# Decode block with attention and MLP: implied semaphore waits left out, a finer last piece of the second MLP matrix, one store from ACT

## The chip, the cores and the metric

The kernel runs on one core of a Trainium2 chip. The metric is the device time in microseconds of one execution; of several runs the median is given, with the lowest and the highest. Beside these runs one execution is profiled; its trace gives the rows shown below.

## What is computed

Eight tokens (B = 8, one position each, D = 576) go through an attention block and an MLP, and a gate mixes the two:

```
g = sigmoid((x * gate_w).sum(-1))
q = x @ wq                                  # 32 heads of 128, 16 heads of K and V
p = softmax(q . k / sqrt(128))              # over the last 2048 of 8192 cached positions
a = (p . v) @ wo                            # wo: 4096 x 576
b = gelu(layernorm(x) @ w1 + b1) @ w2 + b2  # w1: 576 x 4608, w2: 4608 x 576
out = g * a + (1 - g) * b
```

All inputs are bfloat16. The cached keys and values that are read (2 x 64 MiB) are most of what is moved; the four weight matrices make up most of the rest.

## The kernel before

**The planner.** The kernel is written as a list of operations (`_Op`), each with an engine, a function that issues it, the operations that it depends on (`deps`), operations that it must only be issued after (`after`), and a guessed cost. `_Plan.schedule()` (line 62) plays the list through with these costs, takes at each step the operation that can start first, and so fixes the order of each engine: ACT, POOL, DVE, PE, and SP, which issues almost all transfers. It also gives each operation a planned start and end (`t0`, `t1`). Then each operation that another one depends on gets a number on its engine's semaphore (`milestone`, lines 129 to 139); a transfer counts 16 on a semaphore of its own.

**The waits.** `emit` (line 141) walks one engine's order. For each dependency it issues a `wait_ge` (line 153), unless this engine has already waited for the same semaphore at that value or a higher one (`known`). It doesn't see that a wait for one operation may already say that another is done: because the other stands earlier on the same engine, or because the one waited for has itself waited for the other. An operation with several dependencies on one engine, in rising order, so gets a wait for each of them.

**The stream.** Transfers run through nine slots of 2 MB in SBUF. A K unit (line 635, 32 of them) is four batches of one KV head: one transfer, two transposes on DVE (line 653), score matmuls (line 667) into four PSUM banks. Four K units make a group; `softmax` (line 595) then takes the maxima over the row (598), brings three quarters of the partitions to the first (601), takes maxima of these (602, 603, 604), writes the scaled negative to four places (607), and runs four exponentials on ACT (612) and four transposes on DVE (617); the sums go through 620 to 623 and 629. A V unit (line 679, 32) is one transfer, 16 matmuls (690), an evacuation by ACT (696), eight small matmuls that gather the result (701), and after every second unit another ACT evacuation (711) and a product on POOL (719). After eight V units `wo_chunk` (722) brings in a quarter of `wo`, arranges rows by matmul (734), evacuates them by ACT (738) and adds 16 matmuls of the projection.

The stream's order is five K units, then K and V in turn with the `wo` quarters in between; when the K units are used up, V units 27 to 31, the last quarter of `wo`, the bias (line 746) and the second MLP matrix `w2` in four blocks (`m2_chunk`, line 754). A block has 9 weight rows for each partition and takes 18 matmuls. The first three blocks come by one transfer each; the last comes in pieces of 4, 3 and 2 rows, each with its own semaphore. Projection, bias and `w2` all add into one PSUM bank through `AccGroup` (line 543, matmuls at line 552): each weight row is a pair of matmuls of 288 columns, the left half of the output to partitions 0 to 7 and the right half to partitions 32 to 39.

**The end.** When all groups have added up, DVE copies the left half (line 779) and ACT the right half (780) to `out_sb`, at partitions 0 and 32, and each half is stored by a transfer of its own, from SP and from ACT (782). SP waits for both (`final_wait`, 783).

Each engine has one queue in order. A wait blocks what stands behind it on its engine.

Of the kernel before, what the change touches and what calls it, by code (L numbers as in the profile page):

```python
# [6 lines left out]
BF = mybir.dt.bfloat16  # L7
# [5 lines left out]
ENGS = ("sp", "act", "pool", "dve", "pe")  # L13
# [25 lines left out]
class _Plan:  # L39
# [10 lines left out]
    def add(self, eng, fn, deps=(), name=None, cost=0.1, after=(), prio=0):  # L50
        op = _Op(eng, fn, deps, name, cost, after=after, prio=prio)
        op.idx = len(self.all)
        self.all.append(op)
        return op

    def dma(self, eng, fn, semkey, nbytes, deps=(), name=None, after=(), prio=0):
        op = _Op(eng, fn, deps, name, self.DMA_ISSUE, after=after, is_dma=True, dma_sem=semkey, nbytes=nbytes, prio=prio)
        op.idx = len(self.all)
        self.all.append(op)
        return op  # L60

    def schedule(self):
        n = len(self.all)
        done = [False] * n
        eng_free = {e: 0.0 for e in ENGS}
        dma_free = 0.0
        remaining = set(range(n))
        npred = [0] * n
        succ = [[] for _ in range(n)]
        for op in self.all:  # L70
            preds = set(d.idx for d in op.deps) | set(d.idx for d in op.after)
            npred[op.idx] = len(preds)
            for p in preds:
                succ[p].append(op.idx)
        ready = [i for i in range(n) if npred[i] == 0]
        count = 0
        while ready:
            best = None
            best_key = None
            for i in ready:  # L80
                op = self.all[i]
                r = 0.0
                for d in op.deps:
                    r = max(r, d.t1 + self.SEM_LAT)
                for d in op.after:
                    r = max(r, d.t0)
                est = max(eng_free[op.eng], r)
                key = (est - 0.2 * op.prio, -op.prio, i)
                if best_key is None or key < best_key:
                    best_key = key  # L90
                    best = i
            op = self.all[best]
            ready.remove(best)
            est = max([eng_free[op.eng]] + [d.t1 + self.SEM_LAT for d in op.deps] + [d.t0 for d in op.after])
            op.t0 = est
            if op.is_dma:
                eng_free[op.eng] = est + op.cost
                if op.nbytes < 65536:
                    op.t1 = est + 0.4 + self.DMA_LAT
                else:  # L100
                    start = max(est + 0.4, dma_free)
                    dma_free = start + op.nbytes / self.DMA_BW
                    op.t1 = dma_free + self.DMA_LAT
            else:
                op.t1 = est + op.cost
                eng_free[op.eng] = op.t1
            op.pos = len(self.order[op.eng])
            self.order[op.eng].append(op)
            done[best] = True
            count += 1  # L110
            for s_ in succ[best]:
                npred[s_] -= 1
                if npred[s_] == 0:
                    ready.append(s_)
        assert count == n, "dependency cycle in plan"
        self.makespan = max(op.t1 for op in self.all)
        prev = None
        for op in self.order["pool"]:
            narrow = op.name.startswith("qr")
            if prev is not None and narrow != prev.name.startswith("qr"):  # L120
                op.deps.append(prev)
            prev = op
        cnts = {}
        for e in ENGS:
            for op in self.order[e]:
                if op.is_dma:
                    cnts[op.dma_sem] = cnts.get(op.dma_sem, 0) + 1
                    op.dma_val = 16 * cnts[op.dma_sem]
        needed = set()
        for op in self.all:  # L130
            for d in op.deps:
                if not d.is_dma:
                    needed.add(d.idx)
        for e in ENGS:
            c = 0
            for op in self.order[e]:
                if op.idx in needed:
                    c += 1
                    op.milestone = c
# [32 lines left out]
def build_kernel(nc, A_x, A_k_cache, A_v_cache, A_wq, A_wo, B_x, B_w1, B_b1, B_w2, B_b2, gate_w, out):  # L172
    B, Sq, D = A_x.shape
# [12 lines left out]
    FC, FJ = 4, 9  # L186
# [6 lines left out]
    JN = D // NJ  # L193
    BIG = 1.0e9
    x2 = A_x.rearrange("b s d -> (b s) d")
    out2 = out.rearrange("b s d -> (b s) d")

    with ExitStack() as es:
# [5 lines left out]
        def req(name, nelem, dt, align=64):  # L204
            sz = 2 if dt == BF else 4
            o = aoff[0] + ARENA_BASE
            o = (o + align - 1) // align * align - ARENA_BASE
            R[name] = (o, nelem, dt)
            aoff[0] = o + nelem * sz
# [35 lines left out]
        req("oX", 2 * WO_CH * WO_CH * 8, BF)  # L245
        req("oP", 2 * WO_CH * 8, BF)
        req("o32", 2 * 16, F32)
        req("out_sb", JN, BF)
        req("PT", 2 * 2048, BF)
        req("P", 2048, BF)  # L250
        req("osb", 2 * 512, F32)
# [24 lines left out]
        def view(name, parts=128):  # L276
            o, n, dt = R[name]
            a = arena[0:parts, o // 2: o // 2 + (n * (2 if dt == BF else 4)) // 2]
            if dt == F32:
                a = a.bitcast(F32)  # L280
            return a
# [31 lines left out]
        out_sb = view("out_sb")  # L313
# [10 lines left out]
        def slot(s):  # L324
            return RAW[:, s * SE:(s + 1) * SE]
# [11 lines left out]
        ps = es.enter_context(nc.psum_tensor("ps", [128, 8, 512], F32))  # L337
# [5 lines left out]
        BK_ACC = 7  # L343
# [6 lines left out]
        add, dma = P.add, P.dma  # L350
# [43 lines left out]
        for s in range(2):  # L394
            o_xz.append(add("dve", (lambda s=s: lambda e: e.tensor_copy(xz[:, s, :].rearrange("p (k z) -> p k z", z=2)[:, :, s], x_sb[:, 512:576]))(),  # L395
                            deps=dx + [o_xz0], name="xz%d" % s, cost=0.12))
# [12 lines left out]
        for s in range(2):  # L409
            o_yz.append(add("dve", (lambda s=s: lambda e: e.tensor_copy(yz[:, s, :].rearrange("p (k z) -> p k z", z=2)[:, :, s], y_bf[:, 512:576]))(),  # L410
                            deps=[o_y, o_yz0], name="yz%d" % s, cost=0.12))
# [30 lines left out]
        def b1ev_fn(e):  # L442
# [5 lines left out]
                   deps=[o_dga, o_dgb, o_onesf], name="g_pe", cost=0.4, after=[o_yTp])  # L448
# [7 lines left out]
        for q in range(4):  # L456
            o_i32.append(add("dve", (lambda q=q: lambda e: e.tensor_copy(i32[32 * q:32 * q + 32, :], ident[32 * q:32 * q + 32, 32 * q:32 * q + 32]))(),
                             deps=[o_ident, o_obl], name="i32_%d" % q, cost=0.15, prio=-1))
# [3 lines left out]
                     deps=[o_ident, o_obl], name="mskt", cost=0.25, prio=-1)  # L462
# [110 lines left out]
        last_dma = [d_w1r]  # L573
# [16 lines left out]
        def take_slot():  # L590
            n = n_slot[0]
            n_slot[0] += 1
            return (n + 6) % NSLOT
# [160 lines left out]
        def m2_chunk(ci):  # L754
            s = take_slot()
            dst = slot(s)[:, 0:FJ * D]
            src = B_w2[FCW * ci:FCW * ci + FCW, :].rearrange("(p j) n -> p (j n)", j=FJ)
            cuts = [0, 4, 7, 9] if ci == FC - 1 else [0, FJ]
            ops = []
            for n, (j0, j1) in enumerate(zip(cuts, cuts[1:])):  # L760
                d = dma("sp", (lambda j0=j0, j1=j1: lambda e: e.dma_start(dst[:, j0 * D:j1 * D], src[:, j0 * D:j1 * D]))(),
                        ("t%d" % n) if ci == FC - 1 else ("s%d" % s), 128 * (j1 - j0) * D * 2, deps=slot_free[s] if n == 0 else [], name="d_w2_%d_%d" % (ci, n), after=last_dma[-1:])
                last_dma.append(d)
                mms = [(hT[:, FJ * ci + j, :], dst[:, j * D:(j + 1) * D]) for j in range(j0, j1)]
                ops.append(AccGroup("m2_%d_%d" % (ci, n), mms, [o_hT, d], cost=0.25 * (j1 - j0), after=o_m2[-1:]).op)
                o_m2.append(ops[-1])
            slot_free[s] = ops

        pv_hist = []
        for kind, i in stream:  # L770
            {"K": k_unit, "V": v_unit, "W": wo_chunk, "M": m2_chunk, "B": bias}[kind](i)

        acc_ops = [g_.op for g_ in acc_groups]
        fin = []
        for j, (eng, ev) in enumerate((("sp", "dve"), ("act", "act"))):
            def ev_fn(e, j=j, ev=ev):
                dst, src = out_sb[32 * j:32 * j + 8, :], ps[32 * j:32 * j + 8, BK_ACC, 0:JN]
                if ev == "dve":
                    return e.tensor_copy(dst, src)  # L779
                return e.activation(out=dst, in_=src, func=ACTF.Copy)  # L780
            o_fin = add(ev, ev_fn, deps=acc_ops, name="fin%d" % j, cost=0.4, prio=9)
            fin.append(dma(eng, (lambda j=j: lambda e: e.dma_start(out2[:, JN * j:JN * j + JN], out_sb[32 * j:32 * j + 8, :]))(), "out" if j == 0 else "outb", 8 * JN * 2, deps=[o_fin], name="d_out%d" % j, after=last_dma[-1:]))
        add("sp", lambda e: None, deps=fin, name="final_wait", cost=0.05)

        P.schedule()
# [67 lines left out]
```

## Time and profile before

| what | value |
|---|---|
| median of 3 runs | 369.81 us (368.82 to 369.83) |
| the profiled execution | 369.34 us |
| its span, first to last instruction | 367.6 us |
| granted TensorE clock, mean | 0.838 |
| bytes moved, rate over the span | 154.62 MB, 421 GB/s |
| busy: PE, DVE, ACT, POOL | 268.4, 212.1, 48.8, 42.3 us |

How to read the rows of the profile: PE is the TensorE matmul, PEld its weight load, DVE the VectorE, ACT the ScalarE, POOL the GpSimd and SP the SyncE; a q behind the name (PEldq, ACTq) is that engine's queue, with instructions that don't count as work (waits, issues of transfers). L153 is line 153 of the kernel. A chain is the work that ended last, followed back from the end: each row has its start, its length and what it is; "issue" in it is time in which the engine waited for nothing that the profile shows. The slices cut the span into 40 equal parts and give busy shares in tenths; PEclk is the clock that TensorE was granted, in tenths of full speed. In rows of a line, three numbers with slashes are the least, median and greatest duration in ns.

### The profile page before, as it was taken

What the parts mean: (1) busy time and instruction counts of PE and PEld (TensorE: products, weight loads), DVE (VectorE), ACT (ScalarE), POOL (GpSimd) and SP (SyncE); (2) the same over time, 40 slices, a digit from 0 to 9 for tenths busy, and PEclk for the clock granted to TensorE, in tenths of its full rate; (3) what the DMA queues carried; (4) which work ended last, traced back from release to release, by engine and by line L of the source; (5) the groups of instructions that cost most, each with busy time, mean ns of one, the idle gap of its engine ahead of it and who ended that gap; (6) DMA issues with size and microseconds to landing.
All of it is one profiled execution on the core that took longest, in us unless ns stands there. A gap on an engine that the chain in (4) does not pass through costs nothing.

```text
span 367.6 us, 4620 instructions
## 1 busy us (share of the span) xinstructions
PE 268.4 (73%) x1869; PEld 132.4 (36%) x1869; DVE 212.1 (58%) x254; ACT 48.8 (13%) x122; POOL 42.3 (12%) x166
## 2 busy tenths in 40 slices
PE   0349984699598498874986488875987489684887
PEld 0339431244244243332432243322433244232454
DVE  0804599699687764459744754469644874464000
ACT  1010000201300310003000300003000310004110
POOL 8020011012012001010111010010111000000000
PEclk9999998599799878887898878887888788985558
DMA  8999999999999999999999999999999999999993
GB/s 345 428 417 428 430 431 431 431 428 430 428 433 430 425 436 430 428 431 431 431 435 430 420 437 431 427 431 435 428 426 430 437 429 427 426 430 437 421 428 158
DMA packets 11341, 154.62 MB, mean 421 GB/s; under 512 B 1292, under 2 KB 1332, under 8 KB 1976
## 3 DMA queue, kind: packets, MB, share of 16 engines
q1 hardware_dynamic: 11264, 154.29, 98.4%
q8 instruction: 15, 0.25, 0.2%
q10 hardware_dynamic: 56, 0.03, 0.0%
q14 instruction: 6, 0.05, 0.0%
HBM read 154.31 MB, written 0.01 MB: 420 GB/s over the span
## 4 chain that ended last, share of the span: by engine, by line
DMA 58%; PE 20%; DVE 16%; issue 4%; ACT 1%; POOL 1%; SPq 0%; POOLq 0%; DVEq 0%; ACTq 0%
DMA arena<-in_A_k_cache_dram 51%; DVE arena L653 12%; PE ps L667 9%; DMA arena<-in_B_w_dram 7%; PE ps L552 2%; PE ps L509 2%; DVE arena L598 2%; PE ps L690 2%; PE ps L701 2%; PE ps L663 1%; DVE arena L617 1%; PE ps L511 1%; DVE arena L607 0%; DVE arena L601 0%; ACT arena L696 0%
## 5 line engine op out<-in xcount | busy, mean ns | idle before, releaser
L653 DVE STREAM_TRANSPOSE arena<-arena 128x2048 f32<-128x2048 f32 x64 | 145.1, 2296 | 71.8 <-DMA arena<-in_A_k_cache_dram 68.2
L667 PE MATMUL ps<-arena 128*128 128x512 bf16 x512 | 151.7, 453 | 17.2 <-DVE arena L653 17.1
L667 PEld LDWEIGHTS ps<-arena 128*128 128x128 bf16 x512 | 53.8, 112 | 107.0 <-issue 41.1
L646 POOL COPY arena<-arena 32x32 bf16<-32x32 bf16 x128 | 26.0, 203 | 215.4 <-PE ps L667 200.8
L701 PE MATMUL ps<-arena 128*128 128x8 f32 x256 | 37.2, 272 | 15.4 <-ACT arena L696 15.4
L701 PEld LDWEIGHTS ps<-arena 128*128 128x128 f32 x256 | 35.9, 214 | 29.3 <-ACT arena L696 28.0
L696 ACT ACTIVATE arena<-ps 128x512 f32<-128x512 f32 x32 | 19.1, 598 | 191.6 <-PE ps L690 191.6
L663 PE MATMUL ps<-arena 128*128 128x512 bf16 x32 | 14.9, 621 | 33.7 <-DVE arena L617 29.0
L690 PE MATMUL ps<-arena 128*32 128x512 bf16 x512 | 37.1, 413 | 0.7 <-ACT arena L711 0.7
L598 DVE TENSOR_REDUCE arena<-ps 128x1 f32<-128x2048 f32 x8 | 18.3, 2282 | 18.0 <-PE ps L667 18.0
L612 ACT ACTIVATE arena<-ps,arena 128x512 bf16<-128x512 f32 x32 | 21.6, 686 | 41.8 <-DVE arena L607 41.8
L617 DVE STREAM_TRANSPOSE arena<-arena 128x512 bf16<-128x512 bf16 x32 | 19.8, 674 | 0.9 <-ACT arena L612 0.9
L719 POOL TENSOR_TENSOR arena<-arena 128x128 bf16<-128x128 f32 x16 | 8.1, 509 | 91.5 <-ACT arena L711 90.7
L690 PEld LDWEIGHTS ps<-arena 128*32 128x32 bf16 x512 | 11.3, 100 | 18.8 <-issue 12.5
L663 PEld LDWEIGHTS ps<-arena 128*128 128x128 bf16 x32 | 3.5, 127 | 39.4 <-DVE arena L617 35.0
L779 DVE CAST arena<-ps 8x288 bf16<-8x288 f32 x1 | 0.4, 445 | 29.1 <-PE ps L552 29.1
L509 PE MATMUL ps<-arena 128*128 128x8 bf16 x144 | 10.9, 201 | 4.7 <-DMA arena<-in_B_w_dram 4.7
L552 PE MATMUL ps<-arena 128*8 128x288 bf16 (+1 forms) x140 | 12.7, 348 | 1.3 <-ACT arena L738 1.3
L509 PEld LDWEIGHTS ps<-arena 128*128 128x128 bf16 x144 | 10.8, 159 | 5.2 <-DMA arena<-in_B_w_dram 5.2
L623 DVE RECIPROCAL arena<-ps 128x32 f32<-128x32 f32 x8 | 2.9, 358 | 13.4 <-PE ps L622 13.4
L422 PE MATMUL ps<-arena 8*128 8x8 bf16 x8 | 0.5, 167 | 13.5 <-DVE arena L395 9.8
L552 PEld LDWEIGHTS ps<-arena 128*8 128x8 bf16 (+1 forms) x140 | 6.8, 99 | 5.2 <-ACT arena L738 1.8
(88 smaller groups left out, 97.7 us busy)
## 6 DMA issues: line engine op xcount, KB each, us to landing
arena<-in_A_k_cache_dram SPq DMA_DIRECT2D x32, 2048.0 KB, 35.2
arena<-in_A_v_cache_dram SPq DMA_DIRECT2D x32, 2048.0 KB, 36.5
arena<-in_B_w_dram SPq DMA_DIRECT2D x1, 4608.0 KB, 24.2
arena<-in_A_wo_dram SPq DMA_DIRECT2D x4, 1152.0 KB, 35.8
arena<-in_A_wq_dram SPq DMA_DIRECT2D x1, 4096.0 KB, 12.9
arena<-in_B_w_dram SPq DMA_DIRECT2D x3, 1296.0 KB, 33.6
arena<-in_B_w_dram SPq DMA_DIRECT2D x2, 576.0 KB, 28.5
arena<-in_A_wq_dram SPq DMA_DIRECT2D x1, 512.0 KB, 3.3
```

What stands on the lines that cost most here:

```text
L509: ins = e.matmul(out_, lhsT, yT[:, kt, :], start=(kt == 0), stop=False)
L552: ins = e.matmul(ps[32 * j:32 * j + 8, BK_ACC, 0:JN], lhsT, rhs[:, JN * j:JN * j + JN], start=False, stop=True, skip_group_check=True, til ...
L598: mx = add("dve", lambda e: e.tensor_reduce(out=k(MX), in_=ps[:, 0:4, :].rearrange("p a n -> p (a n)"), axis=AXL.X, op=ALU.max), deps=[qk_ ...
L612: return e.activation(out=Pm[:, 512 * c:512 * c + 512], in_=ps[:, c, :], func=ACTF.Exp, bias=k(NB), scale=SCALE, accum_out=k(SUM + c))
L617: pts.append(add("dve", (lambda c=c: lambda e: e.transpose(bass.AP(arena, offset=aoffs("PT") + (g % 2) * 2048 + 128 * c, ap=[[AST, 128], [ ...
L646: return e.tensor_copy(dst, src)
L653: tr = add("dve", (lambda h=h, kb=kb: lambda e: e.transpose(bass.AP(arena_f, offset=foffs("KT") + kb * 2048, ap=[[AST // 2, 128], [1, 2048]]),
L663: mm = e.matmul(ps[:, rc, :], maskL, maskR, start=True, stop=False)
L667: mm = e.matmul(ps[:, rc, :], qbd[:, ub, 2 * h + ee, :], rhs, start=False, stop=(q == 3 and h == 1 and ee == 1))
L690: mm = e.matmul(ps[32 * t:32 * t + 32, BK_OS[i % 2], :], PT[:, g % 2, q, 32 * r4:32 * r4 + 32], slot(s)[:, 512 * r4:512 * r4 + 512], start ...
L696: o_ev[i] = add("act", lambda e: e.activation(out=osb[:, i % 2, :], in_=ps[:, BK_OS[i % 2], :], func=ACTF.Copy), deps=[prev] + ([o_sel[i - ...
L701: mm = e.matmul(ps[:, BK_OS[i % 2], 0:8], osb[:, i % 2, 128 * r:128 * r + 128], i32[:, 8 * r:8 * r + 8], start=(r == 0), stop=(r == 3), sk ...
```

## The change

Three edits.

1. Between planning and numbering, `schedule()` now thins out the dependencies. It walks the engines' orders and keeps for each operation a table of what is known to be done when it is done: the highest position on each engine and the highest count on each transfer's semaphore. An operation inherits the table of the one before it on its engine (what had been waited for by then) and of each dependency that is kept. A dependency is dropped when the inherited table covers it or another kept one does. The dependencies are gone through from the one planned to end last to the one planned to end first, and stay in that order. Only operations that are still waited for get a semaphore number.
2. The last block of `w2` comes in pieces of 4, 3, 1 and 1 rows.
3. `out_sb` is twice as wide; DVE and ACT write the two halves side by side on partitions 0 to 7, and one transfer from ACT stores all of it, after both.

```diff
+        key = lambda d: ("dma", d.dma_sem) if d.is_dma else ("eng", d.eng)
+        val = lambda d: d.dma_val if d.is_dma else d.pos + 1
+        last = {e: {} for e in ENGS}
...
+        def covers(vc, d):
+            return vc.get(key(d), 0) >= val(d)
...
+                    vc = last[e]
+                    keep = []
+                    for d in sorted(op.deps, key=lambda d: -d.t1):
+                        if covers(vc, d) or (d.eng == e and not d.is_dma and any(covers(seen[o.idx], d) for o in keep)):
+                            continue
+                        if any(covers(seen[o.idx], d) for o in keep):
+                            continue
+                        keep = [o for o in keep if not covers(seen[d.idx], o)] + [d]
+                    op.deps = keep
+                    vc = dict(vc)
+                    for d in keep:
+                        for s_, v in seen[d.idx].items():
+                            vc[s_] = max(vc.get(s_, 0), v)
+                    last[e] = vc
+                    done_vc = dict(vc)
+                    done_vc[key(op)] = max(done_vc.get(key(op), 0), val(op))
+                    seen[op.idx] = done_vc
...
-        req("out_sb", JN, BF)
+        req("out_sb", D, BF)
...
-            cuts = [0, 4, 7, 9] if ci == FC - 1 else [0, FJ]
+            cuts = [0, 4, 7, 8, 9] if ci == FC - 1 else [0, FJ]
...
-        for j, (eng, ev) in enumerate((("sp", "dve"), ("act", "act"))):
+        for j, ev in enumerate(("dve", "act")):
             def ev_fn(e, j=j, ev=ev):
-                dst, src = out_sb[32 * j:32 * j + 8, :], ps[32 * j:32 * j + 8, BK_ACC, 0:JN]
+                dst, src = out_sb[0:8, JN * j:JN * j + JN], ps[32 * j:32 * j + 8, BK_ACC, 0:JN]
...
-            o_fin = add(ev, ev_fn, deps=acc_ops, name="fin%d" % j, cost=0.4, prio=9)
-            fin.append(dma(eng, (lambda j=j: lambda e: e.dma_start(out2[:, JN * j:JN * j + JN], out_sb[32 * j:32 * j + 8, :]))(), "out" if j == 0 else "outb", 8 * JN * 2, deps=[o_fin], name="d_out%d" % j, after=last_dma[-1:]))
+            fin.append(add(ev, ev_fn, deps=acc_ops, name="fin%d" % j, cost=0.4, prio=9))
+        fin = [dma("act", lambda e: e.dma_start(out2, out_sb[0:8, :]), "out", 8 * D * 2, deps=fin, name="d_out", after=last_dma[-1:])]
         add("sp", lambda e: None, deps=fin, name="final_wait", cost=0.05)
```

More of the change, by code (lines that the diff above doesn't have):

```diff
@@ L128, in schedule @@
                     op.dma_val = 16 * cnts[op.dma_sem]
+        key = lambda d: ("dma", d.dma_sem) if d.is_dma else ("eng", d.eng)
+        val = lambda d: d.dma_val if d.is_dma else d.pos + 1
+        last = {e: {} for e in ENGS}
+        heads = {e: 0 for e in ENGS}
+        seen = {}
+        def covers(vc, d):
+            return vc.get(key(d), 0) >= val(d)
+        left = n
+        while left:
+            for e in ENGS:
+                while heads[e] < len(self.order[e]):
+                    op = self.order[e][heads[e]]
+                    if any(d.idx not in seen for d in op.deps):
+                        break
+                    vc = last[e]
[15 more added lines that the diff above has]
+                    seen[op.idx] = done_vc
+                    heads[e] += 1
+                    left -= 1
         needed = set()
```

## The prediction

> **What bounds the kernel now.** I read the page first (its slices, then the chain), then the chain of waits in order of time, then the last 30 us by windows and by the timeline.
>
> ```profile
> span 367.6 us, 4620 instructions
> PE   0349984699598498874986488875987489684887
> PEclk9999998599799878887898878887888788985558
> DMA  8999999999999999999999999999999999999993
> DMA 58%; PE 20%; DVE 16%; issue 4%; ACT 1%; POOL 1%; SPq 0%; POOLq 0%; DVEq 0%; ACTq 0%
> 282.26 37.04 DMA arena<-in_A_k_cache_dram
> ...
> 357.54 7.69 PE ps L552 x88
> ```
>
> The DMA row is full from the second slice to the last but one: the transfers bound the kernel until the last K unit lands at 282.26 + 37.04 = 319.3 us. Behind it the chain holds no transfer any more. It runs through that unit's transposes, scores and softmax, four V units on PE and ACT, and one closing burst of 88 matmuls of L552: the last output projection (16) and all of the second MLP matrix (72). So from 319.3 us on this is a compute tail of 46 us, and only what shortens that tail can move the end. The PEclk row shows it at half clock (5) in slices 37 to 39.
>
> ```profile
> 358.00:359.00 1.00, 1.00 (x12) 0.57 (x10) 0.50 0.98 410
> 358.00:361.00 3.00, 3.00 (x28) 1.70 (x26) 0.50 0.94 389
> 361.00:362.00 1.00, 1.00 (x14) 0.55 (x10) 0.00 (x0) 0.00 (x0) 0.00 (x0) 0.55 0.59 236
> 362.00:363.00 1.00, 1.00 (x22) 0.74 (x18) 1.00 0.47 173
> 362.00:364.00 2.00, 2.00 (x38) 1.48 (x34) 1.00 0.29 107
> ```
>
> Below, the issues of the second matrix's transfers (duration in ns, first and last start), the size and time to landing of its last piece, and the last pair of matmuls:
>
> ```profile
> L761 SPq DMA_DIRECT2D arena<-in_B_w_dram x6: 327/356/5926, 317.2 to 333.0; - x6
> arena<-in_B_w_dram SPq DMA_DIRECT2D x1, 288.0 KB, 30.8
> 364.92 0.29 PE L552 MATMUL ps<-arena 128*8 128x288 bf16 x2
> ```
>
> In the windows the first number after the stretch is its length, then busy time and count for PE and for its weight loads; the last three are granted clock, DMA share and GB/s. At clock 0.50 two more microseconds (358:361 against 358:359) bring 16 more matmuls, so a pair (one weight row) takes 0.25 us; at 1.00 one more microsecond brings 16, so 0.125 us. The clock of 0.55 in 361:362 puts the rise 0.1 us before that window's end, at 361.9. Check: (361.9 - 357.54)/0.25 = 17.4 pairs, the other 26.6 take 3.3 us, together 7.7, as the chain has it. The last piece of the matrix (288 KB, 2 rows) was issued at 333.0 and took 30.8 us, so it landed at 363.8. The last pair starts at 364.92, the pair before it one step earlier at 364.8: PE reaches the last piece **1.0 us after it landed**. The burst is bound by its start and by the clock, not by the transfer.
>
> **The change part by part.**
>
> *Waits left out.* A wait that does not fit on its instruction stands ahead of it as an instruction of its own, at L153:
>
> ```profile
> L153 PEldq EVENT_SEMAPHORE  x87: 51/51/2942, 9.5 to 356.7; - x87
> L153 DVEq EVENT_SEMAPHORE  x47: 21/21/50, 9.1 to 365.3; - x47
> L153 SPq EVENT_SEMAPHORE  x33: 17/17/17, 41.0 to 367.0; - x33
> L153 ACTq EVENT_SEMAPHORE  x33: 17/17/38, 63.9 to 365.3; - x33
> L153 POOLq EVENT_SEMAPHORE  x26: 17/17/43, 15.5 to 337.4; - x26
> ```
>
> That is 226 in all. Those ahead of 319.3 us are hidden by the full DMA queue; SP's are hidden because its transfers wait over 30 us in the queue. If that cover were gone, they would cost at most what those in the tail cost each, below 0.2 us. What counts is an L153 instruction between a release and the chain's next step:
>
> ```profile
> 329.63 0.05 issue
> ...
> 329.83 0.03 issue
> 329.86 0.02 DVEq L153
> ...
> 329.92 0.16 DVE arena L604
> 330.08 0.02 issue
> 330.11 0.14 DVE arena L607
> ...
> 330.79 0.02 issue
> 330.81 0.04 ACTq L153
> ...
> 330.89 0.27 ACT arena L612
> ...
> 337.32 0.14 issue
> ...
> 340.01 0.04 issue
> ...
> 356.40 0.24 issue
> ...
> 365.23 0.03 issue
> 365.26 0.05 DVEq L153
> ...
> 365.35 0.45 DVE arena L779
> ```
>
> - L604 (maximum of two maxima) waits for two earlier DVE operations; the later one covers the other. Its gap of 0.09 falls to the 0.03 that L607 shows: **0.06**. L603 ahead of it also loses one, in a gap of 0.05 at 329.63; there I take nothing, for it also has to follow L602.
> - L612 (the exponentials) waits for four DVE results in a row; the last covers all. Gap 0.11 to the 0.03 of a plain hand-over: **0.08**.
> - L690 for V unit 28, and alike for 30, waits for its slot's transfer and for ACT. Neither implies the other, both waits stay: 0, at most 0.10 each if their order on the queue turns (0.14 at 337.32 against the 0.04 ahead of L701 at 340.01), and as much lost elsewhere if an order turns the wrong way.
> - L734 (rows of the last projection) waits for four GpSimd results, a DVE and more; the fourth product (L719) covers them all, being behind them on its engine or having waited for them. Gap 0.24 to the 0.04 of a plain hand-over to PE: **0.20**.
>
> So the burst starts 0.06 + 0.08 + 0.20 = 0.34 us earlier. How much reaches the end hangs on the clock. If the rise comes as much earlier as the burst, all 0.34; if it stays at 361.9, the pairs gained are pairs at half clock, done otherwise at full clock, and only half, 0.17, is left. Between executions the rise moves anyway, so I take the full 0.34 as the mean. The Trainium skill, "VectorE: DVE Perf Modes", section "The DRAIN you can't avoid", speaks against the first term: eight VectorE copies took the same time with a semaphore after each as with one after the last. By it the L604 term is nothing and the sum 0.06 us smaller; the trace here has the 0.09 against 0.03 above.
>
> *Last block in pieces of 4, 3, 1, 1.* The bytes are the same. One more transfer is issued by SP (0.33 to 0.36 us at L761, while over 30 us of work lies queued), one more wait stands on a weight load, and the pairs are the same. It lets PE begin the last row but one sooner, but PE comes 1.0 us after the whole has landed: 0 gained. Smaller rows may land later; the 1.0 us (0.7 to 0.8 after the gain above) hides that. If the cover went (a burst over 0.8 us earlier), the end would be the last landing plus one pair instead of two: 0.12 us less.
>
> *The store.* Both evacuations now write the same 8 partitions, and one transfer from ACT waits for both.
>
> ```profile
> 365.77 0.30 ACTq L782 DMA_DIRECT2D out_dram<-arena  x1
> 365.82 0.32 SPq L782 DMA_DIRECT2D out_dram<-arena  x1
> ...
> SPq L153 <- DMA out_dram<-arena: 0.9, 1, 0.9
> SPq L198 <- DMA out_dram<-arena: 0.2, 1, 0.2
> L153 SPq EVENT_SEMAPHORE  x1: 17/17/17, 367.0 to 367.0; - x1
> ```
>
> The evacuations wait today for a list of PE groups, one L153 behind the other; the last costs the gap 365.23 to 365.35. With one wait each they start 0.09 earlier, so DVE's ends at 365.71 instead of 365.80 and ACT issues at about 365.74. Behind the waiting transfer nothing else is queued on ACT, and only SP's final wait needs it. Today ACT's half lands at 367.0 (first wait) and SP's 0.2 later, though it was issued only 0.06 later: SP's half is what ends the kernel. ACT's took 367.0 - 365.77 = 1.23; from 365.74 the whole lands at 366.97 against 367.2: **0.23**. One store of 1152 B rows isn't in the trace; from below it takes ACT's 1.23, from above SP's 1.38 (then 0.08 is left); I take 1.23, its own queue's. The wider `out_sb` moves later buffers and issues nothing.
>
> **Sum:** 0.34 + 0.23 = 0.57 us. The profiled execution took 369.34 (span 367.6 and 1.7 around it), so **368.8**. It lies 0.47 under the median of the runs, 369.81, in the middle of their 368.82 to 369.83.
>
> **Rivals.**
> - *The clock rises later* (the slower side). Place: the burst. Price: 0.5 us for each microsecond that half clock holds longer. Decides: from 2.1 us later on, (0.47 + 0.57)/0.5, the result is over 369.81 and from 4.3 us on over 370.9. At half clock to the end the burst takes 44 x 0.25 = 11.0 instead of 7.7: 372.1. I take 3 us later, under half of what is possible (11.0 - 4.4): 368.8 + 1.5 = 370.3. For it: the PEclk row holds half clock from slice 37 (331 us) on, though PE works in most of it (4, 8 and 8 tenths in slices 37 to 39 of its row), and the runs differ by 1 us. Against: nothing in the change makes PE less busy.
> - *The clock rises earlier.* Then the end is the last landing: 363.8 plus a pair of 0.29, near 364.1 instead of 365.23, so 1.1 + 0.23 less: 368.0. For it: the same 1 us between runs.
>   The Trainium skill, "TensorE: Matmul & The Clock Gate", "What's actually happening", has the clock set by a free-running window of 3413 ns that does not start with the kernel. By that the rise would come 3.4 to 6.8 us after the burst's start (an estimate from that page) where this trace has 4.4, which is 0.5 us less to 1.2 us more at the end. No single trace can show the phase.
> - *The waits cost nothing* (the gaps stay, as hand-over time): only the store's 0.14 to 0.2 is left, 369.15.
> - *The extra piece lands late.* A transfer alone takes 1.23 to 1.38 us (the stores); added to 363.8 that is at most 365.2, plus a pair 365.5, 0.3 later than today: 369.4 with the store's gain. Against it: the pieces are issued over 30 us before they land, so what is fixed in a transfer passes beside the queue ahead of it. The Trainium skill, "DMA: Bandwidth & Descriptors", "Anatomy of one DMA", fits 2.0 us fixed for each transfer on another issuing path; by it the end would be 370.0.
>
> **How the numbers follow.** Forecast 0.52 (by itself 368.4 to 369.3: half the burst's gain lost or the two L690 gaps won, and a rise moved by half a microsecond either way), clock later 0.17, clock earlier 0.15, waits free 0.11, late piece 0.05. The predicted time is the forecast's, 368.8. A measurement of this kernel can tell about 0.3% from no change: the bounds about 369.81 are 368.7 and 370.9. Faster: the earlier clock's 0.15 and under four tenths of the forecast, 0.19: 0.34. Slower: a third of the later clock and a little for the late piece, 0.07. Same: 0.59. The range takes in the earlier clock from 368.0 and most of the later one: 368.0 to 370.1.
>
> **What would show it.** Right: no L153 between L603 and L604, ahead of L612, L734, L779 and L780; the gap ahead of L734 near 0.04; far fewer than 226 of them; one store from ACT landing 1.2 to 1.3 us after its issue; the pairs of the burst still at 0.25 and 0.125 us. Wrong: a PE gap inside the burst (the transfer decides), L153 instructions still at these places, or a burst whose clock rises at another distance from its start than 4.4 us, which alone can outweigh everything above.

## The result, and the profile after

The changed kernel takes **369.04 us** (median of 22 runs, 368.17 to 370.49) against 369.78 us (22 runs, 368.79 to 370.94) before: ratio 0.9979, 95% interval 0.997 to 0.9988. That is 0.74 us less in the median, faster, but by less than 0.3%. The forecast was 368.8, with "same" (within 0.3% of no change) as the likeliest outcome. The profiled execution took 369.03 us.

The page's first line and the chain of the changed kernel; its line numbers are 35 higher behind the planner (L633 is the maximum, L638 and L639 the maxima of two, L642 the scalings, L647 the exponentials, L769 the rows of the last projection, L587 the burst):

```profile
span 367.3 us, 4489 instructions
```

```profile
326.84 2.30 DVE arena L633
...
329.90 0.02 issue
329.92 0.16 DVE arena L639
...
330.73 0.02 issue
330.75 0.79 ACT arena L647 x2
...
337.18 0.04 issue
...
356.07 0.04 issue
356.12 0.62 PE ps L769 x8
...
357.04 8.03 PE ps L587 x88
365.07 0.02 issue
365.09 0.45 DVE arena L814
```

No wait instruction is left in these gaps. Ahead of L639 stand 0.02 us instead of 0.09, ahead of the exponentials 0.02 instead of 0.11, ahead of V unit 28 0.04 instead of 0.14, ahead of L769 0.04 instead of 0.24, ahead of the evacuations 0.02 instead of 0.12. The burst starts at 357.04 instead of 357.54. Yet PE ends only 0.16 us earlier, because the burst takes 8.03 us instead of 7.69. The windows say why (length, PE and weight loads busy, the other three engines, clock, DMA share, GB/s):

```profile
361.00:362.00 1.00, 1.00 (x12) 0.54 (x8) 0.00 (x0) 0.00 (x0) 0.00 (x0) 0.50 0.59 228
362.00:363.00 1.00, 1.00 (x19) 0.73 (x16) 0.00 (x0) 0.00 (x0) 0.00 (x0) 0.95 0.40 153
```

0.95 in 362:363 puts the rise at 362.1, where it was 361.9 before: the burst came 0.5 us earlier, the rise 0.2 us later. With a pair at 0.25 us at half clock and 0.125 at full, 44 pairs end at half the start plus half the rise plus 5.5 us: 0.5 x 357.04 + 0.5 x 362.1 + 5.5 = 365.07, as the chain has it. So of the earlier start half, 0.25 us, was gained, and the later rise took 0.1 of that.

The wait instructions that are left:

```profile
L188 PEldq EVENT_SEMAPHORE  x43: 51/51/4610, 37.4 to 356.1; - x43
L188 DVEq EVENT_SEMAPHORE  x22: 21/21/21, 2.3 to 314.0; - x22
L188 POOLq EVENT_SEMAPHORE  x22: 17/17/17, 83.0 to 337.2; - x22
L188 ACTq EVENT_SEMAPHORE  x8: 17/17/17, 113.4 to 365.5; - x8
```

95 instead of 226, none on SP. And the end, by the timeline:

```profile
365.09 0.45 DVE L814 CAST arena<-ps 8x288 bf16<-8x288 f32 x1 [28.95 <-PE ps L587]
365.58 0.29 ACTq L817 DMA_DIRECT2D out_dram<-arena  x1
```

The store starts 0.51 us after PE's end, where SP's started 0.59 after it. From PE's end to the span's end it is 367.3 - 365.07 = 2.23 us, before 367.6 - 365.23 = 2.37.

### The profile page after: what moved, and what is told of

Read it like the earlier page. It is cut to its first block, busy times and chain, and to the rows that moved or that the text cites. A ratio compares the mean times of both kernels' runs of the same rounds, so it can differ in the third digit from the quotient of the medians.

```text
span 367.3 us, 4489 instructions
## 1 busy us (share of the span) xinstructions
PE 268.1 (73%) x1869; PEld 131.8 (36%) x1869; DVE 211.6 (58%) x254; ACT 48.8 (13%) x122; POOL 42.4 (12%) x166
## 4 chain that ended last, share of the span: by engine, by line
DMA 58%; PE 21%; DVE 14%; issue 3%; ACT 2%; POOL 1%; SPq 0%; POOLq 0%
DMA arena<-in_A_k_cache_dram 51%; DVE arena L688 10%; PE ps L702 9%; DMA arena<-in_B_w_dram 7%; PE ps L587 3%; PE ps L544 2%; DVE arena L633 2%; PE ps L725 2%; ACT arena L647 2%; PE ps L736 2%; PE ps L698 1%; DVE arena L652 1%; PE ps L546 1%; DVE arena L642 0%; DVE arena L636 0%
## 5 line engine op out<-in xcount | busy, mean ns | idle before, releaser
L633 DVE TENSOR_REDUCE arena<-ps 128x1 f32<-128x2048 f32 x8 | 18.3, 2281 | 21.1 <-PE ps L702 21.1
L647 ACT ACTIVATE arena<-ps,arena 128x512 bf16<-128x512 f32 x32 | 21.6, 686 | 39.1 <-DVE arena L642 39.1
L754 POOL TENSOR_TENSOR arena<-arena 128x128 bf16<-128x128 f32 x16 | 8.1, 508 | 91.7 <-ACT arena L746 91.1
L587 PE MATMUL ps<-arena 128*8 128x288 bf16 (+1 forms) x140 | 13.0, 355 | 1.3 <-ACT arena L773 1.3
L587 PEld LDWEIGHTS ps<-arena 128*8 128x8 bf16 (+1 forms) x140 | 7.0, 102 | 5.8 <-ACT arena L773 1.8
```

The costliest lines, as they stand in the source:

```text
L587: ins = e.matmul(ps[32 * j:32 * j + 8, BK_ACC, 0:JN], lhsT, rhs[:, JN * j:JN * j + JN], start=False, stop=True, skip_group_check=True, til ...
L633: mx = add("dve", lambda e: e.tensor_reduce(out=k(MX), in_=ps[:, 0:4, :].rearrange("p a n -> p (a n)"), axis=AXL.X, op=ALU.max), deps=[qk_ ...
L647: return e.activation(out=Pm[:, 512 * c:512 * c + 512], in_=ps[:, c, :], func=ACTF.Exp, bias=k(NB), scale=SCALE, accum_out=k(SUM + c))
```

## The experiments

My theory, with the trace of after in hand: the waits shorten the chain from the last maximum to the burst, in every execution alike, by 0.59 us (the maximum starts at 326.84 and the burst 30.20 us later; before 326.75 and 30.79), and the end by 0.1; the store gives the rest, the pieces nothing; and the clock, which moves between executions, adds or takes its own part. The rivals: the store is the gain; the extra piece costs; or it's the number of waits that counts, not their place.

### The three edits alone

*Waits alone* is the thinning put into the kernel before, unchanged otherwise.

> Only the thinning of the waits; pieces 4, 3, 2 and two stores as before. Theory (the waits are nearly all of the gain): the burst of L552 starts 0.5 us earlier than before's 357.5, give or take 0.1 by the clock, the gap ahead of the evacuations falls from 0.12 to 0.02, and the ratio is 0.9981 (0.7 us less). Rival (the single store is the gain, waits only shift where engines idle): burst at the same time, ratio 1.000.

Measured: 369.24 us (11 runs) against 369.80, ratio 0.9976 (0.9965 to 0.9988).

*Store alone*: the end of the changed kernel in the kernel before.

> Only the single store from ACT; all waits and pieces as before. Theory: the last evacuation still ends 0.57 us after PE's end; the store takes 1.31 us from issue to landing against 1.38 of SP's today, and begins no earlier than DVE's end, so span and time change by 0.05 to 0.1 us, ratio 0.9998. Rival (the store's half of the gain as predicted): 0.23 us less, ratio 0.9994. The two ratios can't be told apart by time; the rows of the end can.

Measured: 369.62 us (12 runs), ratio 0.9995 (0.9981 to 1.0008). By the rows of the end PE ends at 365.60 and the store is issued at 366.20, 0.60 us later, where SP's was issued 0.59 later before. From PE's end to the span's end it is 367.9 - 365.60 = 2.30 us, against 2.37 before and 366.6 - 364.37 = 2.23 with waits alone, which is the changed kernel's 2.23 as well. Spans are given to 0.1 us, so the store by itself is worth 0.1 us at most, as the theory had it.

*Pieces alone*:

```diff
-            cuts = [0, 4, 7, 9] if ci == FC - 1 else [0, FJ]
+            cuts = [0, 4, 7, 8, 9] if ci == FC - 1 else [0, FJ]
```

> Only the pieces 4, 3, 1, 1; all else as before. Theory: PE reaches the last piece 0.7 us or more after it landed, the burst has no gap, ratio 1.000. Rival (a transfer more costs at the end): the last landing comes 0.3 us or more later and PE waits for it, ratio 1.001 or more. Rival (the pieces give the gain): ratio 0.999 or less.

Measured: 370.35 us (11 runs), ratio 1.0007 (0.9991 to 1.0023).

In time only the first stands clear of one. The chains of the profiled executions are sharper. From the chain of waits alone, of store alone and of pieces alone, the last maximum and the burst (start and length; it ends at their sum):

```profile
325.97 2.30 DVE arena L633
356.17 8.20 PE ps L587 x88
```

```profile
328.03 2.30 DVE arena L598
358.81 6.79 PE ps L552 x88
```

```profile
327.98 2.30 DVE arena L598
358.77 8.30 PE ps L552 x88
```

From maximum to burst it is 30.20 us with the waits thinned, and 30.78 and 30.79 without: 0.59 us, the same in two pairs of executions. The starts themselves differ by up to 2 us. That is the clock in the score matmuls ahead of the maximum, at 321.7 to 325.9 us of waits alone and of store alone:

```profile
321.70:325.90 4.20, 3.94 (x20) 1.42 (x24) 2.19 (x1) 0.00 (x0) 0.00 (x0) 1.00 1.00 425
```

```profile
321.70:325.90 4.20, 4.20 (x11) 1.38 (x11) 2.03 (x1) 0.00 (x0) 0.00 (x0) 0.50 1.00 429
```

20 matmuls against 11 in the same time. So one profile beside another can be out by more than the whole change; steps between two points of one chain are not. The burst's own length goes by the same rule in each of them, with the rise worked out from the clock of the window that holds it:

| kernel | burst starts | clock, in window | rise | end by the rule | end in the chain |
|---|---|---|---|---|---|
| before | 357.54 | 0.55 in 361:362 | 361.9 | 365.2 | 365.23 |
| changed | 357.04 | 0.95 in 362:363 | 362.1 | 365.1 | 365.07 |
| waits alone | 356.17 | 0.82 in 361:362 | 361.4 | 364.3 | 364.37 |
| store alone | 358.81 | 0.84 in 361:362 | 361.3 | 365.6 | 365.60 |
| pieces alone | 358.77 | 0.82 in 364:365 | 364.4 | 367.1 | 367.07 |

Pieces alone has the longest of the bursts at 8.30 us and ends last; its weight loads and matmuls have no gap, and PE ends 3 us behind the transfers (DMA share 0.00 in 364:365), so it isn't the extra transfer that was late, but the clock. The window of pieces alone in which its clock rose:

```profile
364.00:365.00 1.00, 1.00 (x16) 0.71 (x14) 0.00 (x0) 0.00 (x0) 0.00 (x0) 0.82 0.00 0
```

### What makes a wait cheap

*Sorted only*: no dependency is dropped, the lists are put in the order that the change uses.

```diff
+        for op in self.all:
+            op.deps = sorted(op.deps, key=lambda d: -d.t1)
         needed = set()
```

> No dependency is dropped; each operation's dependencies are only put in order of planned end, the latest first, so that one wait on an engine's later number makes the list's earlier numbers of that engine needless, and the latest wait is the one that stays on the instruction. Theory (what counts is which wait stands last before the instruction, not how many there are): most of the thinning's gain, the gap ahead of the rows of the last projection near 0.04 instead of 0.24, that ahead of V unit 28 near 0.05 instead of 0.14, ratio 0.9983, though waits as instructions of their own remain. Rival (the number of waits counts): gaps shrink only as far as the number of wait instructions does, ratio near 0.999 to 1.000.

Measured: 368.98 us (11 runs), ratio 0.9979 (0.9966 to 0.9992). Its chain, with the maximum at L600, the gap ahead of V unit 28 at 338.52 and that ahead of the last projection's rows at 357.41:

```profile
328.11 2.30 DVE arena L600
...
338.52 0.04 issue
...
357.41 0.05 issue
...
358.38 7.10 PE ps L554 x88
```

From maximum to burst 30.27: sorting gave 0.52 of the 0.59 us. But it changes more than the order. A wait for an engine's highest number makes `known` skip the lower ones, and of the 226 wait instructions 112 are left, not many more than the changed kernel's 95: those of PE below, 26 each on DVE and POOL, 14 on ACT and 1 on SP.

```profile
L155 PEldq EVENT_SEMAPHORE  x45: 51/51/8274, 1.8 to 357.5; - x45
```

The latest wait is now issued first, and the number of waits has halved; this run doesn't tell the one from the other, and its rival stands. The next run keeps the number at 95 and turns the order alone.

*Order reversed*: the changed kernel, with what is kept issued the other way round.

```diff
-                    op.deps = keep
+                    op.deps = keep[::-1]
```

> The changed kernel, but the dependencies that are kept are issued in the opposite order, the one planned to end first in front. Theory (the first wait stays on the instruction, so the order decides what still has to pass after the late release): the gap ahead of V units 28 and 30 is 0.14 again instead of 0.05, those with a single wait stay as in the changed kernel; from the maximum's end to the burst's start 28.1 us (27.9 in the changed kernel, 28.5 before). Rival (the order is indifferent): 27.9.

Measured: 369.55 us (12 runs), ratio 0.9996 (0.9977 to 1.0014). The chain of this kernel:

```profile
325.96 2.30 DVE arena L633
...
329.87 0.79 ACT arena L647 x2
...
336.30 0.14 issue
...
355.48 0.05 issue
...
356.40 0.14 issue
356.54 1.60 PE ps L587 x11
```

V unit 28's gap is 0.14 again (336.30), as forecast, and so is V unit 30's. The gap ahead of those rows, 0.05 at 355.48, stays, and so does the stretch from the maximum to the exponentials, 329.87 - 325.96 = 3.91 us as in the changed kernel. From maximum to burst it is 30.58, 0.38 more than in the changed kernel and more than the 0.2 expected: the last projection ahead of the burst has two waits as well (0.14 at 356.40 instead of 0.04), which I had not counted, and the last product on POOL (L754) starts 2.29 us after the gathering matmuls before it, 2.17 in the changed kernel.

So, as far as these rows show, of two waits the first in the list stays on the instruction and the other has to pass ahead of it; the place of the late one costs 0.1 us on PE each time. The order is not indifferent: turned the wrong way, with as many wait instructions (95), it takes back 0.38 us. Of that only the 0.20 at V units 28 and 30 is gain undone; the other 0.2 is lost at places where the kernel before lost nothing (0.04 ahead of its burst). And what stays when the order is turned, the rows' gap and the exponentials, goes with the waits and counts left out. My theory, place and not number, was half of it: of the 0.59 us some 0.20 hangs on the order, the rest on what no longer has to be waited for at these places or counted.

*All counts kept*: the changed kernel, where every operation that counted before still counts.

```diff
+        needed = set()
+        for op in self.all:
+            for d in op.deps:
+                if not d.is_dma:
+                    needed.add(d.idx)
         key = lambda d: ("dma", d.dma_sem) if d.is_dma else ("eng", d.eng)
...
-        needed = set()
-        for op in self.all:
-            for d in op.deps:
-                if not d.is_dma:
-                    needed.add(d.idx)
```

> The changed kernel, but every operation that counted on its engine's semaphore before still counts, though nobody waits for that number any more. Theory (a count costs a little on DVE too): the four scalings of L642 take 0.67 us again instead of 0.62 and the three copies of L636 0.49 instead of 0.47, so the maximum's end to the burst's start is 27.97 instead of 27.91. Rival (a count is free, the waits were all): 0.62 and 27.91.

Measured: 368.27 us (12 runs), ratio 0.9971 (0.9957 to 0.9984). The timelines of this kernel, then of the changed one:

```profile
326.08 2.29 DVE L633 TENSOR_REDUCE arena<-ps 128x1 f32<-128x2048 f32 x1 [2.07 <-PE ps L702]
328.40 0.49 DVE L636 COPY arena<-arena 32x1 f32<-32x1 f32 x3
329.36 0.67 DVE L642 TENSOR_SCALAR arena<-arena 32x1 f32<-32x1 f32 x4
356.35 1.12 PE L587 MATMUL ps<-arena 128*8 128x288 bf16 x8 [0.31 <-ACT arena L773]
```

```profile
329.17 0.47 DVE L636 COPY arena<-arena 32x1 f32<-32x1 f32 x3
330.10 0.62 DVE L642 TENSOR_SCALAR arena<-arena 32x1 f32<-32x1 f32 x4
```

0.67 and 0.49 again: a count costs such a DVE operation some 16 ns, and maximum to burst is 30.27 instead of 30.20. Both as forecast. Its time is nonetheless lower than the changed kernel's, which these steps don't explain; the two intervals overlap (0.9957 to 0.9984 and 0.997 to 0.9988), and the clock spreads single runs of either kernel by more than 1 us. In the profiled run the clock was up early, in 359:360, and the end is set by a transfer: its chain closes with the landing of the last piece and one pair of matmuls.

```profile
339.14 24.76 DMA arena<-in_B_w_dram
...
363.94 0.31 PE ps L587 x2
```

That run took 368.24 us, and 9 of the 12 lie between 368.17 and 368.37. Of the changed kernel's 22 runs 9 lie between 368.17 and 368.48, the others from 368.94 up. So more runs of this kernel seem to end with the transfer; why the clock should be up early more often in it, or whether that is chance, stays open.

### Where the floor is

*V unit 27 early*: its evacuation goes ahead of the last exponentials on ACT, and its gathering matmuls ahead of the sum on PE.

```diff
...
             o_sel[i] = add("pe", sel_pv, deps=deps, name="osel%d" % i, cost=1.3, prio=3)
+            if i == 27:
+                for ex in exp_done[7]:
+                    ex.after.append(o_ev[27])
+                sum_pe[7].after.append(o_sel[27])
```

> The changed kernel with one order turned: V unit 27's evacuation goes ahead of the last group's exponentials on ACT, and its gathering matmuls ahead of the sum on PE, so that they fill PE's idle time in the softmax. Theory (the end is set by the compute tail, with the last landing as a floor): exponentials 0.4 us later, V unit 28 some 1.75 us earlier, the burst from about 355.3; the end of PE then comes from the last landing, 363.85 plus one pair, near 364.2, in nearly all runs: 368.2 us with less spread, ratio 0.9955. Rival (the clock gives it back: a longer softmax gap, half clock longer): end of PE at 365 or later, ratio 0.998 or more.

Measured: 368.28 us (12 runs, 368.06 to 368.61) against 369.79 (368.64 to 371.02), ratio 0.9967 (0.9955 to 0.9979).

*Fillers*: matmuls into a bank that nobody reads any more, in PE's waits.

```diff
+        def filler(name, n, after, bank=0, deps=()):
+            def fn(e):
+                mm = None
+                for _ in range(n):
+                    mm = e.matmul(ps[:, bank, 128:512], ident, ones_bf[:, 0:384], start=True, stop=True, skip_group_check=True)
+                return mm
+            return add("pe", fn, deps=list(deps), name=name, cost=0.2 * n, after=after, prio=9)
...
+            if i >= 27:
+                filler("fa%d" % i, 8 if i == 27 else 2, [prev], BK_S if i == 27 else 0, [rc_last[-2]] if i == 27 else exp_done[7])
...
+            if i == 29 or i == 31:
+                filler("fb%d" % i, 1 if i == 29 else 2, [o_sel[i]], 0, exp_done[7])
```

> The changed kernel with extra matmuls that nobody reads, in PE's waits: 8 of 384 columns in the last softmax, 2 after each of V units 28 to 31, 1 and 2 after the gathering of 29 and 31. Theory (half clock in the tail is what makes the tail longer than the transfers, and it comes from PE's idle time): the clock stays or returns to 1.00 between 334 and 355, each V unit takes 2.9 us instead of 4.4, the burst waits for its transfers and ends with the last landing: 368.2 us, ratio 0.9955. Rival (the clock does not answer to so few matmuls): half clock as before and the extra matmuls in the way, 0.3 us each unit at most, ratio 0.998 to 1.002.

Measured: 368.25 us (12 runs, 368.02 to 368.54), ratio 0.9958 (0.9945 to 0.9971).

Both land on the same time with a quarter of the changed kernel's spread (0.5 against 2.3 us): the floor, where the fastest nine runs of the changed kernel lie too. In the chain of V unit 27 early the transfer is back, and in the timeline below it PE waits for it:

```profile
338.98 24.98 DMA arena<-in_B_w_dram
...
364.00 0.31 PE ps L587 x2
```

```profile
364.00 0.09 PEld L587 LDWEIGHTS ps<-arena 128*8 128x8 bf16 x2 [0.28 <-DMA arena<-in_B_w_dram]
364.33 0.40 ACT L821 ACTIVATE arena<-ps 8x288 bf16<-8x288 f32 x1 [8.61 <-PE ps L587]
```

The fillers' mechanism was not what I expected. Windows of that kernel:

```profile
337.00:349.00 12.00, 11.99 (x73) 5.61 (x73) 0.00 (x0) 1.97 (x4) 1.04 (x2) 0.50 1.00 426
349.00:355.00 6.00, 5.24 (x60) 3.27 (x62) 0.00 (x0) 1.00 (x3) 0.50 (x1) 0.98 1.01 430
```

PE was busy for all of 337 to 349, and the clock stayed at 0.50 through it; only then did it rise, so that the last V unit and the burst ran at full clock (the burst started at 354.35; in the changed kernel the rise came at 362.1). The half clock of the tail is thus not explained by PE's idle time as the profile counts it. What the clock goes by stays open here.

*The pieces at the floor*: V unit 27 early, with the last block in pieces of 4, 3, 2 (`cuts = [0, 4, 7, 9]`) or whole (`cuts = [0, 9]`).

> The kernel with V unit 27's evacuation early, with the last block in pieces of 4, 3 and 2 rows. Theory (with the last landing as the bound, what PE still has to do after it counts): PE ends 0.12 us later after the last landing than with the single row, 0.45 instead of 0.33 us; the last landing itself at 363.9, no earlier; 368.4 us, not told apart in time from 368.28. Rival (one transfer less lands earlier): last landing 0.1 us or more earlier, no loss.

> The same, with the last block in one piece of 9 rows. Theory: all 9 pairs of matmuls come after the last landing, 8 x 0.125 more than with a single row; PE ends 1.3 us after the landing instead of 0.33, near 365.2; 369.25 us, ratio 0.9985. Rival (one large transfer lands earlier by what its three fellows cost): half or more of that won back, ratio 0.997.

Measured: 368.21 us (5 runs) with pieces of 4, 3, 2, ratio 0.9958 (0.9946 to 0.9971), not told apart from 368.28; 369.27 us (11 runs) in one piece, ratio 0.9988 (0.9979 to 0.9997). The timelines of the two:

```profile
363.81 0.10 PEld L587 LDWEIGHTS ps<-arena 128*8 128x8 bf16 x4 [0.46 <-DMA arena<-in_B_w_dram]
364.26 0.40 ACT L821 ACTIVATE arena<-ps 8x288 bf16<-8x288 f32 x1 [8.71 <-PE ps L587]
```

```profile
363.78 1.27 PE L587 MATMUL ps<-arena 128*8 128x288 bf16 x18 [1.82 <-DMA arena<-in_B_w_dram]
365.10 0.40 ACT L821 ACTIVATE arena<-ps 8x288 bf16<-8x288 f32 x1 [9.42 <-PE ps L587]
```

The evacuation starts 0.45 us after the 2-row piece is released, 0.33 after the single row (364.00 to 364.33, timeline of V unit 27 early), 1.32 after nine rows. So PE has 0.12 us less left to do behind a single row, as forecast. The landing is not the same, though. In the chains it falls at 338.98 + 24.98 = 363.96 with four pieces (above), at 363.76 with three and at 363.74 with one:

```profile
332.86 30.90 DMA arena<-in_B_w_dram
```

```profile
330.94 32.80 DMA arena<-in_B_w_dram
```

Here the theory missed ("at 363.9, no earlier") and its rival came out: with three pieces the landing is 0.2 us earlier, and nothing is lost (the evacuation starts at 364.26 against 364.33). Part of that is spread between executions: in the traces of all kernels the last landing is at 363.67 to 363.89 with three pieces (five kernels) and at 363.85 to 363.96 with four (six), 0.14 us apart in the mean. So the fourth piece gives PE 0.12 us and costs about as much in landing; at the floor these runs show nothing for it, and in the profile of the changed kernel PE's backlog hides the landing.

## Why the prediction was right

- **What bounds.** Right: behind 319.3 us a compute tail, with the transfers as a floor that it had not reached. V unit 27 early and the fillers show that floor at 368.2 to 368.3, as the rival of the early clock had it (368.0).
- **Waits, 0.34 us: too small, 0.59.** Two things were missed in this term. The order at the two L690 gaps, for which nothing was counted, did turn: 0.10 each, and reversing it brings the gap back. And the counts that are no longer needed are worth 0.07 on DVE, as all counts kept shows. With L604's gap (0.09 to 0.02) and the exponentials' (0.11 to 0.02) the stretch from the maximum's end to the exponentials went from 1.84 to 1.61 us, 0.23 instead of the 0.14 counted. L734's gap fell by 0.20 as worked out; 0.17 of it reached the burst. 0.23 + 0.10 + 0.10 + 0.17 is 0.60, and 0.59 was measured; the two 0.10 are the part that hangs on the order. The rule that speaks against the L604 term (the Trainium skill, "VectorE: DVE Perf Modes", "The DRAIN you can't avoid") did not hold for these short operations (0.14 us each): both the wait and the counts cost DVE time.
- **The store, 0.23 us: too large, 0.14** from PE's end to the span's end. The start came 0.08 earlier as worked out, by the thinned list: with the store alone it came no earlier. The single store did not take ACT's 1.23 us: with the 0.4 us that lie before between the last landing (367.2) and the span's end (367.6), it landed near 366.9, 1.3 after its issue. Of the 0.14, 0.1 is the thinned list ahead of the evacuations, which waits alone has too. The mistake was the choice of the lower bound: the landing, put at 0.15 us sooner (1.23 for 1.38), came 0.1 sooner at most.
- **Pieces: nothing.** Right, by the rows: no gap in the burst, with the extra piece alone or with all of it. For a burst that comes early enough to wait for the transfer the prediction offered 0.12 us; the runs at the floor show a landing about as much later, and nothing gained there either.
- **Sum.** 0.59 + 0.14 = 0.73 against 0.74 in the medians; forecast 0.57. That the forecast came so near is partly luck: two errors of opposite sign. That 0.73 meets 0.74 is no proof either. It takes the whole 0.59 to the end, as the prediction took the whole 0.34 "as the mean"; were the rise to stay where it is, half of it would arrive, 0.30 + 0.14 = 0.44, and the interval of the ratio (0.997 to 0.9988) reaches from 0.44 to 1.1 us. And in runs that end with the transfer an earlier burst brings nothing more. How much of the 0.59 reaches the end on average is not shown.
- **The clock.** The rule of half a microsecond for each that the rise moves holds to 0.1 us in five kernels. The prediction named a rise at another distance from the burst's start than 4.4 us as a sign of being wrong, and in the profile after it came 5.1 us behind it (362.1 - 357.04): 0.7 more, which took 0.35 us of the 0.5. This hid the gain in the pair of profiles: 0.31 us there. By the free-running window of the Trainium skill ("TensorE: Matmul & The Clock Gate", "What's actually happening") I had estimated the rise 3.4 to 6.8 us after the burst's start; in the table it comes 2.5 (store alone) to 5.6 us (pieces alone) after it. A spread of about one window is there; the bounds are not those of the estimate.
- **Late piece, waits that cost nothing.** Both fell: waits alone carries the gain, and where the last piece lands later, by about 0.1 us, PE's backlog or its shorter rest covers it.

## What to carry to other kernels

Look at which wait is released last: make it the one that stays on the instruction, and leave out those that it implies. Sorting a dependency list by its expected end did both and gave nearly all that a full pruning did, 0.52 of 0.59 us, with 112 wait instructions left of 226. Of the 131 wait instructions left out, those ahead of the full transfer queue were worth nothing (the last K unit's transposes start at 319.3 us before and after); in the 46 us tail a handful were worth 0.6 us. And where the clock of one engine moves between executions, compare distances along a chain, not ends: they repeated to 0.01 us here while PE's end moved by more than 2.

## What was not expected of the hardware

- A semaphore count costs a short DVE operation about 16 ns: four scalings take 0.67 us with it on each and 0.62 without, three copies 0.49 and 0.47.
- Of an operation's waits the first issued stays on the instruction and the others pass ahead of it; a late one that has to pass ahead costs PE 0.10 us (0.14 against 0.04, with the same 95 wait instructions in the kernel).
- TensorE stayed at a granted clock of 0.50 for 12 us in which the profile has it busy for 11.99 (the profile models where matmuls end).
